# A recurrent attention and MLP kernel: unit 4's f, q and k turned by DMA transposes, and the first units in another order

## The chip, the cores and the metric

The kernel runs on one core of a Trainium2 chip. The metric is device microseconds of one execution; the time before is the median of seven runs.

## The reference

The input holds q, k, v and f_logit of shape (4, 8, 768, 48): 4 batches, 8 heads, 768 steps, 48 channels. An attention with a state that decays per channel is followed by a normalisation and a two-layer MLP with a residual.

```python
f = 1.0 / (1.0 + np.exp(-f_logit))
for t in range(S):
    state = f[:, :, t, :, None] * state + np.einsum('bhd,bhe->bhde', k[:, :, t], v[:, :, t])
    y[:, :, t] = np.einsum('bhd,bhde->bhe', q[:, :, t], state)
...
xn = (x - mu) / np.sqrt(var + 1e-06) * g_ln
ch = np.maximum(xn @ w_ch1, 0.0) @ w_ch2
return (x + ch)
```

Here x is y with the heads put side by side, (4, 768, 384); w_ch1 is 384 x 1536 and w_ch2 1536 x 384. The weights arrive as 64-bit floats and are turned into 32-bit floats on the chip; everything is computed in float32.

## The kernel before

**Units.** The 768 steps are cut into 12 units of 64 steps; a unit holds all 4 batches, so it has 256 rows for the MLP, and two batches fill the 128 partitions. The loop over units carries `state`. Within a unit the recurrence is written with cumulative products of the gates, made by two scans on VectorE (`after`, line 654, and `upto`, line 666, some 2.3 us each): the scaled k (`kh`, lines 673 and 708) and scaled q (`qh`, lines 673 and 716) give scores (line 751), these are masked (`sc`, line 755) and multiplied with v (line 777); the state of earlier units comes in through `carried` (line 737); `chunk` (line 807) and `state` (line 815) bring the state forward. `kt` (lines 767 and 769) is kh turned back for `chunk`.

**Two ways to get f, q and k with channels on the partitions.** A unit below `DIRECT` loads them as they lie and TensorE transposes them (`across`, line 646): 8 transposes of 128x128 each for f, k and q. A unit from `DIRECT` on takes another way. `split` (lines 424 to 436) lets ScalarE copy each half of the raw tile into two planes of 16-bit halves (line 432) and sends these to DRAM by a DMA on GpSimd's queue (line 436); `transfer` (lines 438 to 449) brings them back by a transposing DMA on SyncE's queue (line 448) into the tiles `turned` and, for k, into the raw tile of q. There is one `turned` for f and q, so the transfers of a unit have to follow each other's readers.

**The MLP.** `turn` (lines 834 to 844) transposes the normalised rows `xn` (line 830) into `xt`. Units 0 and 1 multiply plainly: six tokens of two column blocks of the first layer (`ph`, line 954, relu on ScalarE, line 956), and six tokens of four row blocks of the second (`po`, line 964). From unit 2 on the second layer uses a scheme with seven products (`pp`, line 983), with sums of h (lines 871 to 874) and mixed weights (`mix`, line 581); from unit 3 on the first layer uses a scheme with block products (`bw`, `bx`, `by`, `bz`, `bv`, line 892) and mixed weights (`mix_step`, line 607).

**The weights.** Each of the two matrices comes in 6 pieces of 768 KB. `fetch` issues a piece's DMA on SyncE's queue into one of two buffers (line 530); `read` lets ScalarE take it apart into `upper` and `units` (lines 542 and 543, 0.9 us each), each with two buffers; `write` puts it together on VectorE (lines 551, 554 and 556) and GpSimd (line 558). A piece is named by its first row or column: pieces 0 to 1280 of w1, pieces 0 to 10 of w2.

**What sets the order.** Every engine works through its own instructions in order, and their order is written out by hand in two strings. `START` covers units 0 to 2 and the attention up to unit 4, `UNIT` is repeated for each later unit. `run` (lines 1033 to 1061) goes through the tokens: `a2.q` is a stage of unit 2's attention, `m1` the next step of unit 1's MLP, `l3f` a load (four DMAs on SyncE's queue), `p5k0` a `split` of one half, `x5k` a `transfer`, `f`, `r` and `w` are fetch, read and write of the next weight piece, `d` is an idle matmul that only keeps TensorE busy (line 572), `T` and `t` one third of the mixing of w2 on GpSimd or VectorE, `U` and `u` a step of the mixing of w1, `s` the sums of h and `y` those of xt. A token puts its instructions at the end of the queues of all the engines that it uses, so where a token stands decides what waits behind what on each of them. PSUM gives the transposes and products four single banks in turn, so a product also waits until the reader of an earlier one is done. A DMA on SyncE's queue uses one of eight semaphores in turn and waits for the DMA that used it before.

Of the kernel before, what the change touches and what calls it, by code (L numbers as in the profile page):

```python
# [303 lines left out]


START = """
a0.gates l0k l0q f d a0.after l0x d r l0v d a0.upto
d f a0.kx l1f a0.k a0.kept l1k d a0.q f a0.carried a0.scores
a0.causal a0.values l1x l1q w r d a0.stats a0.kt f a1.gates w
d d a0.norm d a1.after l1v a0.chunk a0.turn f a0.state a1.upto m0  # L310
a1.kept r w a1.kx f a1.k m0 a1.q f r a1.kt r
w a1.carried a1.scores a1.causal d f l2k f l2v f w m0
a1.values r a1.stats l2f r a1.chunk w m0 a1.norm d l2x m0
a1.turn r m0 m1 r w w f w r m1 w
l2q m1 a1.state m1 a2.gates a2.after r m1 a2.kx f m0 m0
r w a2.k l3k w a2.upto a2.kept m1 a2.q m0 m0 m0
m0 a2.carried l3q a2.scores l3v l3f m1 l3x a2.causal U a2.values a2.stats
a2.norm m1 m1 m1 a3.gates m1 m1 a2.kt a2.turn a2.chunk a3.kx m2
m2 l4f a3.after a3.k m2 U a3.upto U T a2.state U a3.q
a3.kept m2 a3.carried a3.scores a3.kt l4v l4k a3.causal U a4.gates U U  # L320
U l4q T t U a3.values a3.chunk a4.after m2 l5f l5v U
a3.stats m2 a4.kx U a3.norm s2 m2 p5f0 a3.state l5k m2 a4.k
U m2 p5f1 m2 a4.kt u a3.turn l6f x5f p5k0 a4.upto a4.q
l4x p5k1 y3 l5q a5.gates m2 m2 l5x a4.kept m2
"""
UNIT = """
a{o}.after m{m} m{m} a{n}.carried a{n}.scores p{o}q0 m{m} a{n}.causal m{m} m{m} m{m} p{o}q1
# [8 lines left out]
def kernel(  # L336
# [19 lines left out]
    nc = tc.nc  # L356
    B, H, S, D = q.shape
    P = 128
    T = 64
# [12 lines left out]
    LEAST = 1e-12  # L372
    PLAIN = 2
    FIRST = 3
    DIRECT = 5
    PIECE = 768

    outer = ctx.enter_context(tc.tile_pool(name="outer", bufs=1))
# [28 lines left out]
    for name, fill in (("f", 40.0), ("q", 0.0), ("k", 0.0)):  # L407
        t = consts.tile([P, G, H, 64], FP32, name=f"{name}raw")
# [9 lines left out]
    halved = {}  # L418

    def raw_of(n, name):  # L420

        return wide_heads["k" if n >= DIRECT and name == "q" else name]

    def split(n, name, g):

        if n >= NU or n < DIRECT:
            return
        if (n, name) not in halved:
            halved[n, name] = drams.tile([P, 2, G, 64 * H], U16, tag=f"{name}halves",
                                         name=f"{name}halves{n}")  # L430
        planes = raws.tile([P, 2, 64 * H], U16, tag="planes", name=f"{name}planes{n}_{g}")
        nc.scalar.copy(  # L432
            out=planes,
            in_=raw_of(n, name)[:, g].rearrange("p h e -> p (h e)").bitcast(U16).rearrange(
                "p (c two) -> p two c", two=2))
        nc.gpsimd.dma_start(out=halved[n, name][:, :, g], in_=planes)  # L436

    def transfer(n, name):

        if n >= NU or n < DIRECT:  # L440
            return
# [188 lines left out]
    def attention(n):  # L630
# [7 lines left out]
        def new(name, shape, **kw):  # L638
            at[name] = work.tile(shape, FP32, tag=name, name=f"{name}{n}", **kw)
            return at[name]  # L640

        def across(src, g):

            pt = one_bank(f"tr{n}")
            for a in range(NP):
                nc.tensor.transpose(pt[:, a * P:(a + 1) * P],  # L646
                                    src[:, g, 2 * a:2 * a + 2].rearrange("p h e -> p (h e)"),
                                    ident)
            return pt.rearrange("p (s t) -> p s t", t=T)
# [20 lines left out]
        def times(dst, pts, by):  # L670
            for g, pt in enumerate(pts):
                segs = slice(g * HS, (g + 1) * HS)
                nc.vector.tensor_tensor(out=dst[:, segs], in0=pt, in1=by[:, segs, 1:E1],
                                        op=ALU.mult)

        def do_gates():
            new("after", [P, NS, E1])
            new("upto", [P, NS, E1])
            new("total", [P, NS], bufs=2)
            if n >= DIRECT:  # L680
                nc.scalar.activation(out=gv[:, :, 1:E1], in_=turned["f"], func=AF.Sigmoid)  # L681
# [17 lines left out]
        def do_k_across():  # L699
            if n < DIRECT:  # L700
                at["pk"] = [across(loaded[n, "k"], g) for g in range(G)]

        def do_k():
            kh = new("kh", [P, NS, T])
            if n < DIRECT:
                times(kh, at["pk"], at["after"])
# [326 lines left out]
    def run(plan):  # L1033
        for token in plan.split():
            kind, rest = token[0], token[1:]
            if kind == "a":
                n, stage = rest.split(".")
                if int(n) >= NU:
                    continue
                if "a" + n not in running:  # L1040
                    running["a" + n] = attention(int(n))
                running["a" + n].pop(stage)()
            elif kind == "m":
                if token not in running:
                    running[token] = mlp(int(rest))
                next(running[token])
            elif kind == "l":
                load(int(rest[:-1]), rest[-1])
            elif kind == "p":
                split(int(rest[:-2]), rest[-2], int(rest[-1]))  # L1050
            elif kind == "x":
                transfer(int(rest[:-1]), rest[-1])
            elif kind == "s":
                sums(int(rest))
            elif kind == "y":
                if FIRST <= int(rest) < NU:
                    sums_of_x(int(rest))
            else:
                {"r": read, "w": write, "f": fetch, "t": mix, "d": idle,
                 "T": lambda: mix(nc.gpsimd), "u": mix_step,  # L1060
                 "U": lambda: mix_step(nc.gpsimd)}[token]()
# [53 lines left out]
```

## Time and profile before

| what | value |
|---|---|
| median of 7 runs | 452.42 us |
| lowest and highest run | 448.65 and 453.76 us |
| the profiled execution | 451.44 us |
| span of its core | 449.7 us |
| around the span | 1.7 us |
| mean granted TensorE clock | 0.992 |
| chain of waits, by engine | PE 90%, DMA 3%, DVE 3% |
| HBM read and written | 30.67 and 15.73 MB |

PE is TensorE's matmuls, PEld its weight loads, DVE VectorE, ACT ScalarE, POOL GpSimd, SP SyncE. A line of a timeline has the start in us, the length in us, engine, source line, operation, output and input, their shapes, how many instructions are merged, and in brackets the idle time before them and what ended it. The chain of waits is followed back from the last instruction; its lines have the start, the length, and what the time went to.

### The profile page before, as it was taken

To read this page: it belongs to the slowest core of one execution; us is meant where nothing else is said; L and a number is where in the kernel's file an instruction comes from. 1 tells how busy PE (TensorE), PEld (TensorE's weight loads), DVE (VectorE), ACT (ScalarE), POOL (GpSimd) and SP (SyncE) were. 2 spreads that over 40 slices of the span, in tenths; PEclk is the share of its full clock that TensorE was granted. 3 is DMA by queue.
4 is the path that set the end of the run, shared out by engine and by line. 5 is a ranking of instruction groups with operands and counts; after the bars stand their busy time and mean duration, and the time that the engine had idled before them with its cause. 6 is when DMAs were issued, how large, how long until landed. Compare 5 with 4: busy or idle time off the path is not lost.

```text
span 449.7 us, 12979 instructions
## 1 busy us (share of the span) xinstructions
PE 432.4 (96%) x5487; PEld 401.8 (89%) x5487; DVE 330.0 (73%) x528; ACT 185.9 (41%) x333; POOL 126.8 (28%) x151
## 2 busy tenths in 40 slices
PE   5789999999999999999999999999999999999994
PEld 4568887667899999999999999999999999999994
DVE  6689878553678987888878878778778788565461
ACT  2266754003234445455454454464464451341320
POOL 2213543249715124124024024024024013011020
PEclk9899999999999999999999999999999999999998
DMA  8989997063645758777876767776778550000001
GB/s 136 196 186 249 244 210 137 20 128 62 121 79 127 182 123 195 153 159 180 148 167 168 152 147 184 159 158 167 160 132 203 118 118 19 21 1 18 20 10 34
DMA packets 173011, 58.36 MB, mean 130 GB/s; under 512 B 160784, under 2 KB 166416, under 8 KB 172944
## 3 DMA queue, kind: packets, MB, share of 16 engines
q1 hardware_dynamic: 167808, 46.03, 51.8%
q0 software_dynamic: 3360, 11.01, 6.8%
q8 instruction: 45, 0.74, 0.7%
q10 hardware_dynamic: 1776, 0.40, 0.5%
q14 instruction: 22, 0.18, 0.1%
HBM read 30.67 MB, written 15.73 MB: 103 GB/s over the span
## 4 chain that ended last, share of the span: by engine, by line
PE 90%; DMA 3%; DVE 3%; SPq 2%; issue 0%; ACT 0%
PE pp L983 30%; PE bx L892 12%; PE ph L954 9%; PE by L892 9%; PE po L964 7%; PE bz L892 4%; PE py L777 3%; PE py L737 3%; PE ps L751 2%; PE kp L767 2%; PE pn L807 2%; PE bv L892 2%; PE tr L646 2%; PE bw L892 2%; SPq L469 2%; PE xp L840 2%
## 5 line engine op out<-in xcount | busy, mean ns | idle before, releaser
L903 ACT ACTIVATE h<-h 128x512 f32<-128x512 f32 x45 | 28.3, 629 | 53.5 <-DVE h L900 47.4
L954 PE MATMUL ph<-xt,w 128*128 128x256 f32 x216 | 48.7, 380 | 0.8 <-ACT xt L842 0.8
L954 PEld LDWEIGHTS ph<-xt,w 128*128 128x128 f32 x216 | 40.4, 190 | 6.5 <-issue 1.0
L983 PE MATMUL pp<-mixed,h 128*128 128x192 f32 x240 | 42.4, 326 | 0.0
L983 PE MATMUL pp<-mixed,s 128*128 128x192 f32 x240 | 42.0, 326 | 0.0
L983 PE MATMUL pp<-w,h 128*128 128x192 f32 x240 | 40.7, 326 | 0.0
L983 PEld LDWEIGHTS pp<-mixed,h 128*128 128x128 f32 x240 | 39.5, 190 | 0.3 <-ACT xt L842 0.3
L983 PEld LDWEIGHTS pp<-mixed,s 128*128 128x128 f32 x240 | 39.1, 190 | 0.0
L983 PEld LDWEIGHTS pp<-w,h 128*128 128x128 f32 x240 | 38.8, 190 | 0.0
L436 POOL DMA_DIRECT2D qhalves<-qplanes x14 | 9.6, 683 | 97.8 <-ACT qplanes L432 97.8
L654 DVE TENSOR_TENSOR_SCAN after<-gates,ends 128x1040 f32<-128x1040 f32 (+1 forms) x13 | 28.7, 2211 | 6.3 <-ACT gates L686 3.4
L900 DVE TENSOR_TENSOR h<-h,bx 128x512 f32<-128x512 f32 x27 | 18.5, 687 | 18.8 <-PE bx L892 18.8
L964 PE MATMUL po<-w,h 128*128 128x384 f32 x96 | 32.0, 488 | 0.0
L666 DVE TENSOR_TENSOR_SCAN upto<-gates,starts 128x1040 f32<-128x1040 f32 (+1 forms) x13 | 30.1, 2314 | 0.4
L892 PE MATMUL bx<-y,v 128*128 128x128 f32 x216 | 29.4, 279 | 0.0
L900 DVE TENSOR_TENSOR h<-h,by 128x512 f32<-128x512 f32 x36 | 24.6, 683 | 6.3 <-PE by L892 5.0
L964 PEld LDWEIGHTS po<-w,h 128*128 128x128 f32 x96 | 17.8, 190 | 11.5
L892 PEld LDWEIGHTS bx<-y,v 128*128 128x128 f32 x216 | 26.2, 192 | 0.5
L681 ACT ACTIVATE gates<-turned 128x1024 f32<-128x1024 f32 x7 | 7.4, 1057 | 44.5 <-DMA turned<-fhalves 42.7
L842 ACT ACTIVATE xt<-xp,gain 128x128 f32<-128x128 f32 x72 | 19.9, 377 | 9.6 <-PE xp L840 9.6
L755 DVE TENSOR_TENSOR sc<-ps,causal 128x1024 f32<-128x1024 f32 x12 | 14.7, 1222 | 11.2 <-PE ps L751 11.2
L558 POOL TENSOR_TENSOR w<-w_0upper,w_0units 128x768 int32<-128x768 int32 x7 | 12.7, 1818 | 31.5 <-DVE w_0upper L556 26.3
(161 smaller groups left out, 960.2 us busy)
## 6 DMA issues: line engine op xcount, KB each, us to landing
w_0words<-in_moe_w_ch_dram SPq DMA_DIRECT2D x7, 768.0 KB, 5.5
kraw<-in_k_dram SPq DMA_DIRECT2D x48, 96.0 KB, 3.6
v<-in_v_dram SPq DMA_DIRECT2D x48, 96.0 KB, 3.0
fraw<-in_f_logit_dram SPq DMA_DIRECT2D x46, 96.0 KB, 3.5
fhalves<-fplanes POOLq DMA_DIRECT2D x14, 256.0 KB, 3.0
khalves<-kplanes POOLq DMA_DIRECT2D x14, 256.0 KB, 2.9
qhalves<-qplanes POOLq DMA_DIRECT2D x14, 256.0 KB, 3.1
kraw<-in_q_dram SPq DMA_DIRECT2D x28, 96.0 KB, 3.2
```

The lines of the kernel that those rows point to most:

```text
L654: nc.vector.tensor_tensor_scan(out=at["after"].rearrange(flat)[:, c0:c1][:, ::-1], data0=gt[:, c0 + 1:c1 + 1][:, ::-1], data1=ends.rearran ...
L666: nc.vector.tensor_tensor_scan(out=at["upto"].rearrange(flat)[:, c0:c1], data0=gt[:, c0:c1], data1=starts.rearrange(flat)[:, c0:c1], initi ...
L737: nc.tensor.matmul(py[half(b), r, e * D:(e + 1) * D], lhsT=qh[head_rows(r), 2 * e + b], rhs=kept[head_rows(r), b, e], start=e == 0, stop=F ...
L755: nc.vector.tensor_tensor(out=new("sc", [P, 2, GA, T]).rearrange("s r e t -> s (r e) t"), in0=at["ps"].rearrange("s r e t -> s (r e) t"), ...
L777: nc.tensor.matmul(py[half(b), r, e * D:(e + 1) * D], lhsT=sc[rows, r, e], rhs=vx[rows, g, a] if r else vt[rows, g, 2 * a], start=n == 0 a ...
L842: nc.scalar.mul(out=xt[:, m, g * P:(g + 1) * P], in_=pt[:, m], mul=gain[:, m:m + 1])
L892: nc.tensor.matmul(banks[bank][:, i], lhsT=right[:, i * P:(i + 1) * P], rhs=left, start=new and i == 0, stop=True, skip_group_check=True)
L900: nc.vector.tensor_tensor(out=out[to], in0=out[to], in1=bank, op=op)
L903: nc.scalar.activation(out=out[to], in_=out[to] if bank is None else bank, func=AF.Relu)
L954: nc.tensor.matmul(ph[:, j], lhsT=w1[:, m, (i + j) * P:(i + j + 1) * P], rhs=xt[:, m], start=m == 0, stop=m == KD - 1)
L964: nc.tensor.matmul(po, lhsT=h[:, i, g * P:(g + 1) * P], rhs=w2[:, i], start=i == 0, stop=i == KF - 1)
L983: nc.tensor.matmul(pp, lhsT=a[:, i], rhs=b[:, i], start=i == 0, stop=i == KH - 1)
```

## The change

Three edits. `DIRECT` is 4 instead of 5: unit 4 is the first whose f, q and k are split and turned by transfers. The DMA that sends the halves to DRAM is issued on ScalarE's queue for that unit; for later units it stays on GpSimd's. And `START` is written anew: it has the splits and transfers of unit 4 (`p4f0` to `p4q1`, `x4f`, `x4k`, `x4q`), no `a4.kx`, 8 idle matmuls instead of 11, `T` three times where it was `T` twice and `t` once, and the other tokens in another order. `UNIT` is the same.

```diff
 START = """
-a0.gates l0k l0q f d a0.after l0x d r l0v d a0.upto
-d f a0.kx l1f a0.k a0.kept l1k d a0.q f a0.carried a0.scores
-a0.causal a0.values l1x l1q w r d a0.stats a0.kt f a1.gates w
-d d a0.norm d a1.after l1v a0.chunk a0.turn f a0.state a1.upto m0
-a1.kept r w a1.kx f a1.k m0 a1.q f r a1.kt r
-w a1.carried a1.scores a1.causal d f l2k f l2v f w m0
-a1.values r a1.stats l2f r a1.chunk w m0 a1.norm d l2x m0
-a1.turn r m0 m1 r w w f w r m1 w
-l2q m1 a1.state m1 a2.gates a2.after r m1 a2.kx f m0 m0
...
-m2 l4f a3.after a3.k m2 U a3.upto U T a2.state U a3.q
-a3.kept m2 a3.carried a3.scores a3.kt l4v l4k a3.causal U a4.gates U U
-U l4q T t U a3.values a3.chunk a4.after m2 l5f l5v U
-a3.stats m2 a4.kx U a3.norm s2 m2 p5f0 a3.state l5k m2 a4.k
-U m2 p5f1 m2 a4.kt u a3.turn l6f x5f p5k0 a4.upto a4.q
-l4x p5k1 y3 l5q a5.gates m2 m2 l5x a4.kept m2
+a0.gates l0k a0.kx l0q d d f a0.after a0.upto l0v l0x r
+f a0.k d d l1f a0.q a0.kept a0.carried d a0.scores a0.causal l1k
+w d a0.values r a0.stats d f l1x a0.kt f l1q a0.norm
+f l1v w a1.gates a1.after a0.chunk a0.turn a0.state f a1.upto r m0
+r a1.kept r a1.kx m0 w a1.k a1.q a1.kt w a1.carried a1.scores
+a1.causal f l2k f m0 w a1.values a1.stats r l2v d f
+l2f w a1.norm m0 m0 f r w f a1.chunk a1.turn m0
+a1.state r r m1 r w f w m1 m1 m1 a2.gates
+w a2.after m0 r l2x w a2.kx r m0 a2.k m1 w
...
+m2 a3.upto m1 p4f1 m1 l4k p4k0 x4f T T U p4k1
+a3.q l4q a2.state T m1 U m2 a3.kept l4v U a3.carried a3.scores
+U U p4q0 a3.kt a4.gates l5f m2 x4k a3.causal a3.chunk U a3.values
+p4q1 a4.after a3.stats l5k l5v m2 U x4q m2 a3.norm s2 a3.turn
+p5f0 m2 U a4.upto m2 p5f1 m2 a3.state a4.k p5k0 a4.q m2
+x5f U a4.kt p5k1 l4x u y3 l5q m2 l5x a4.kept a5.gates
+m2 m2 l6f
 """
...
-    DIRECT = 5
+    DIRECT = 4
...
-        nc.gpsimd.dma_start(out=halved[n, name][:, :, g], in_=planes)
+        (nc.scalar if n == DIRECT else nc.gpsimd).dma_start(out=halved[n, name][:, :, g], in_=planes)
```

More of the change, by code (lines that the diff above doesn't have):

```diff
@@ L306 @@
 START = """
-a0.gates l0k l0q f d a0.after l0x d r l0v d a0.upto
-d f a0.kx l1f a0.k a0.kept l1k d a0.q f a0.carried a0.scores
-a0.causal a0.values l1x l1q w r d a0.stats a0.kt f a1.gates w
-d d a0.norm d a1.after l1v a0.chunk a0.turn f a0.state a1.upto m0
-a1.kept r w a1.kx f a1.k m0 a1.q f r a1.kt r
-w a1.carried a1.scores a1.causal d f l2k f l2v f w m0
-a1.values r a1.stats l2f r a1.chunk w m0 a1.norm d l2x m0
-a1.turn r m0 m1 r w w f w r m1 w
-l2q m1 a1.state m1 a2.gates a2.after r m1 a2.kx f m0 m0
-r w a2.k l3k w a2.upto a2.kept m1 a2.q m0 m0 m0
-m0 a2.carried l3q a2.scores l3v l3f m1 l3x a2.causal U a2.values a2.stats
-a2.norm m1 m1 m1 a3.gates m1 m1 a2.kt a2.turn a2.chunk a3.kx m2
-m2 l4f a3.after a3.k m2 U a3.upto U T a2.state U a3.q
-a3.kept m2 a3.carried a3.scores a3.kt l4v l4k a3.causal U a4.gates U U
-U l4q T t U a3.values a3.chunk a4.after m2 l5f l5v U
-a3.stats m2 a4.kx U a3.norm s2 m2 p5f0 a3.state l5k m2 a4.k
-U m2 p5f1 m2 a4.kt u a3.turn l6f x5f p5k0 a4.upto a4.q
-l4x p5k1 y3 l5q a5.gates m2 m2 l5x a4.kept m2
+a0.gates l0k a0.kx l0q d d f a0.after a0.upto l0v l0x r
[7 more added lines that the diff above has]
+w a2.after m0 r l2x w a2.kx r m0 a2.k m1 w
+a2.upto l3k m1 l2q l3f U l3x a2.q m0 a2.kept m0 m0
+l3q a2.carried a2.scores m0 m1 a2.causal a2.values U a2.stats m1 l3v a3.gates
+a2.kt a2.norm l4f m1 a3.after a2.turn p4f0 a2.chunk a3.kx m2 a3.k U
+m2 a3.upto m1 p4f1 m1 l4k p4k0 x4f T T U p4k1
[5 more added lines that the diff above has]
+m2 m2 l6f
 """
```

## The prediction

> **What bounds the kernel now.** I read the engine shares first, then stretches of 10 us, then the chain of waits, then single engines' timelines.
>
> ```profile
> span 449.7 us, 12979 instructions
> PE 432.4 (96%) x5487; PEld 401.8 (89%) x5487; DVE 330.0 (73%) x528; ACT 185.9 (41%) x333; POOL 126.8 (28%) x151
> ```
>
> TensorE is busy for 432.4 of 449.7 us. The stretches (columns: length, then busy us of PE, PEld, DVE, ACT, POOL, then granted clock, DMA share, GB/s) show where the other 17.3 us lie:
>
> ```profile
> 10.00:20.00 10.00, 7.30 (x151) 6.09 (x150) 8.05 (x14) 2.54 (x4) 1.30 (x1) 0.94 0.88 216
> 20.00:30.00 10.00, 7.48 (x96) 5.49 (x95) 7.39 (x10) 5.58 (x13) 3.35 (x4) 0.89 0.98 192
> 30.00:40.00 10.00, 9.52 (x175) 8.43 (x173) 9.69 (x16) 5.98 (x9) 1.84 (x1) 1.00 0.98 232
> 40.00:50.00 10.00, 10.00 (x173) 8.71 (x165) 9.22 (x14) 7.01 (x10) 6.32 (x5) 1.00 0.65 204
> 50.00:60.00 10.00, 10.00 (x51) 8.84 (x50) 7.01 (x9) 6.44 (x13) 4.32 (x3) 1.00 1.08 260
> 60.00:70.00 10.00, 10.00 (x55) 8.63 (x54) 8.03 (x7) 5.75 (x9) 3.64 (x2) 1.00 1.10 197
> ```
>
> With 5.0 us of idle time in the first 10, 10.7 us are lost before 40 us (and 22 passes of idle matmuls, 0.48 us each in the median, fill part of the rest) and 6.7 after 400. Between, TensorE never waits: there only removed TensorE work, or a new wait, moves the end. Before 40 us the chain shows what the first products wait for:
>
> ```profile
> 15.62 6.93 DMA w_256words<-in_moe_w_ch_dram
> ...
> 25.64 2.28 DVE xn L830 x2
> 27.91 2.24 DVE after L654
> ...
> 30.68 2.33 DVE upto L666
> ```
>
> VectorE works in order: xn of unit 0 stands behind the writing of weight piece 256 and so behind that piece's DMA, though its own input was ready (variance on POOL) at 22.1 us.
>
> I sum at three marks of before: M1, the first product with unit 1's xt (51.65 us); M2, the end of the third token of po (80.15); M3, unit 3's first block product (151.15). After M3 the orders are the same and TensorE is full, so what is won by M3 is won in the end.
>
> **Part 1, to M1: xn of unit 0 ahead of the second piece.** xn takes 2.36 us above, beside a POOL write; a later one takes 0.86 with POOL still. It now fits into VectorE's idle 2.47 us (21.0 to 23.49), ending at 23.0. Then ScalarE sets the pace: units of piece 256 end at 24.27, kt at 25.2, the two gates at 26.2, six xt copies 1.66: the first ph starts at about 27.7 instead of 29.35. On VectorE, after starts at 26.2 (was 27.83), upto ends 31.25, kept 32.1, piece 512 is written by 34.1, kh by 35.3 (was 37.1). Reading piece 512 now stands ahead of the first relu on ScalarE, so it is read at its landing (29.0, issue 23.93 and 5.1) and not at 32.71; piece 1024 is requested at some 31.4 instead of 34.5.
> Then the DMA decides. Piece 1280 landed at 43.6 (issue 38.07, landing 5.5). The same bytes precede it in both orders, and DMA was at 0.98 until 40, so I leave it at 43.6: read (0.9 to the first half), written on VectorE (2.1), xn (2.36, beside POOL again) put xn of unit 1 at 49.0. TensorE comes there at 48.4: ph at 27.7, 31.2, 38.2, 42.3 and 44.9, carried at 36.8, pn to 48.4. So M1 falls at 49.4: **2.25 us won**; 0 if piece 1280 lands 2.25 us later.
>
> **Part 2, M1 to M2: reads ahead of relus.** On ScalarE the reads of w2's pieces 4 and 6 now stand before the relus of unit 1's products 2 to 4. The second half of the f transposes of unit 2 needs the bank of product 2, so it waits for piece 6 of w2. Before, that read began at 61.12, waiting for its DMA:
>
> ```profile
> 61.12 0.93 ACT L542 ACTIVATE w_0upper<-w_0words 128x768 f32<-128x768 f32 x1 [1.88 <-DMA w_0words<-in_moe_w_ch_dram]
> 61.95 0.91 ACT L543 ACTIVATE w_0units<-w_0words 128x768 int32<-128x768 uint32 x1
> 62.75 1.06 ACT L956 ACTIVATE h<-ph 128x512 f32<-128x512 f32 x2
> ```
>
> The relu was over 2.25 us after the landing, and TensorE needed it at 65.0: 1.7 us of cover. Now TensorE comes at 62.75, and f of unit 2 is requested ahead of the piece. From 43.6 on, 4.32 MB are ahead of its landing (four pieces of 0.786, three inputs of 0.393). At 260 GB/s (the stretch 50 to 60, which has this mix) it lands at 60.2; at 197 (60 to 70) at 65.5. I take 250: 60.9, a wait of 0.4. Then q of unit 2 is requested behind k of unit 3, and that behind unit 2's k transposes and the last weight piece: landing about 75.0 against 74.6, another 0.4. M2: **1.45 us won** (78.7).
>
> **Part 3, M2 to M3: unit 4 by transfers.** Removed: 24 transposes, three groups of 8, each 0.87 us from start to start (133.92 to 134.80): 2.6 us off a full TensorE. Added: six ScalarE copies (1.0 each) and six DMA issues on ScalarE (two took 1.42 at the start, 0.71 each), 10.3 us on an engine busy 2.7 to 4.9 of each 10 us between 100 and 150; by my order kt of unit 3 is still copied 1.7 us before pn needs it. If that cover went, pn would wait one for one. Three transfers on SP issue in 2.0 to 2.9 us and land in 4.4 to 5.4 (7.0 at most): by my order f lands 4 us before its sigmoid, k 9 and q 4 before use, with loads in front of them counted. One mix goes from VectorE (2.0) to POOL (4.0): from 16.4 us after M2 POOL has 7 steps of 1.3 and 12 of 1.0, so it ends at 37.5, and the first product that needs them starts 56 after M2. Loads, sigmoids and multiplies keep their lengths (kh 1.27 for two halves, 1.21 whole).
> But a new wait comes. upto of unit 4 moves ahead of kh on VectorE, and the transposes of kh stand after the fourth pp:
>
> ```profile
> 134.75 0.96 DVE L871 TENSOR_TENSOR s<-h 128x768 f32<-128x768 f32 x1 [0.16 <-ACT h L956]
> ...
> 138.77 0.94 DVE L815 TENSOR_TENSOR state<-kept,pn 128x768 f32<-128x768 f32 x1
> 139.63 0.34 DVE L991 TENSOR_TENSOR p1x<-p1x,pp 128x192 f32<-128x192 f32 x1
> 139.90 1.27 DVE L673 TENSOR_TENSOR kh<-tr,after 128x512 f32<-128x512 f32 x2
> ```
>
> From the end of unit 2's last ph: sums from 0.83 to 4.85, upto 2.73 (160.66 to 163.39), two adds 0.54, state 0.87, kh 1.2: 10.2. TensorE has xp 0.7 and four pp 7.8 and stands at 8.5. It waits 1.7 us. Net of part 3: **0.9 won**, 2.6 without that wait.
>
> **The three idle matmuls less, and k ahead of others.** The granted clock fell to 0.50 from 19 to 22 us, after gaps; kp took 1.91 us there and 1.04 warm. With three idles less between f of unit 1 and pn, TensorE is busy about 3.1 of the 4.3 us before the first ph. If that ph ran slower by 1.91 to 1.04 it would cost 2.2 us, of which 0.6 are covered by xn of unit 1; at 1.00 nothing. I take nothing, since the clock recovered by itself after 22 us.
> [...]
>
> **Sum.** 1.45 + 0.9 = 2.4 us: 449.0 in the profiled execution's terms (451.44). That one lies 1 us below the median of the seven runs, 452.42; the forecast for a median is **450.0**. A measurement can tell about 0.5% (2.3 us) from no change.
>
> **Rivals.**
> 1. *The waits do not come* (w2 lands at 60, kh is ready by 8.5 us): for, the 260 GB/s stretch; against, VectorE's order, which is fixed. 2.25 + 2.6 = 4.9 won: 447.6.
> 2. *Only the transposes pay*: the first ph runs cold or piece 1280 is 1.5 us late, so 0 to 0.5 is left at M2; with 0.9 that is 451.3. For: clock 0.50; against: clock 1.00 from 25 us.
> 3. *Slower: TensorE waits for piece 6 of w2 through the relus.* At 197 GB/s it lands at 65.5, the wait is 5.0 and the late last piece delays q by 0.6: 2.25 - 5.6 + 0.9 = -2.4, so 454.9. It decides below some 215 GB/s (landing after 63.7). For: 192 and 197 in two stretches full of inputs; against: those carried more small inputs.
> 4. *ScalarE's queue holds the transfers*: if q's transfer is over 4 us late, VectorE stops at qh with the adds behind it; each us costs one. It ends on rival 3's side. That the change does not do what it says is out: in the built order unit 4 has no transposes of f, k and q.
>
> **Chances.** Forecast 0.40, rival 1 0.15, rival 2 0.25, rival 3 0.16, rival 4 0.04. Most of the forecast's case, and rival 1, lie beyond 0.5%: faster 0.48; same 0.32 (rival 2 and the forecast's shallow side); slower 0.20. The range runs from rival 1, less 0.9 for the spread of the runs, to rival 3: 446.7 to 454.9.
>
> **What would show it.** First ph near 27.7; M1 near 49.4; f transposes of unit 2 split by a wait of under 1 us; no unit 4 transposes of f, k and q; a wait of about 1.7 us ahead of kp of unit 4, put down to kh; M3 near 148.8 and 33.2 us per unit as before. I am wrong if TensorE waits over 2 us for a relu near 63 us, if a transfer is what VectorE waits for near 140, or if the stretch 20 to 35 shows a clock below 0.89.

## The result and the profile after

The changed kernel takes 454.05 us in the median of 25 runs against 451.27 us of 62 runs of the kernel before: a ratio of 1.0063, interval 1.0048 to 1.0078. A second measurement gave 453.94 against 452.14 us, 1.0034 (1.0002 to 1.0065). The two medians differ by 0.6% and 0.4%, and both intervals lie above 1: it is slightly slower, where 450.0 and faster had been forecast. Each ratio and its interval compare the two sets of runs and can differ a little from the quotient of the two medians. The profiled execution has a span of 451.9 us (449.7 before). First the page of the changed kernel, then its stretches with the columns of the prediction:

```profile
span 451.9 us, 12930 instructions
PE 432.0 (96%) x5457; PEld 400.1 (89%) x5457; DVE 334.4 (74%) x522; ACT 191.8 (42%) x338; POOL 131.8 (29%) x155
```

```profile
20.00:30.00 10.00, 8.84 (x107) 7.17 (x100) 7.79 (x11) 7.69 (x17) 4.98 (x4) 0.75 1.23 249
...
140.00:150.00 10.00, 6.99 (x37) 6.72 (x36) 9.93 (x14) 3.16 (x4) 5.08 (x7) 0.83 0.46 120
```

TensorE has fewer matmuls and is busy as long as before (432.0, 432.4). The stretch from 140 us shows why: TensorE idles for 3.0 us and has a granted clock of 0.83 of full speed, while VectorE is busy for 9.93 of 10. The marks divide the difference:

| distance, us | before | changed |
|---|---|---|
| start to M1 | 51.65 | 51.77 |
| M1 to M3 | 99.50 | 101.37 |
| M3 to the end | 298.55 | 298.76 |

M1 is the first product behind the transposes of unit 1's xn; the instruction there is unit 0's last first-layer product, so it is a mark and not a reader of xt. Nothing is won up to M1 (2.25 was forecast), and 1.87 us are lost from M1 to M3, where about 0.1 was to be won (0.9 less the two waits of 0.4).

**Up to M1.** The early xn came as forecast: 0.87 us instead of 2.36, and the scan `after` started at 26.32 (26.2 forecast). Right behind it the gain was lost. VectorE, then GpSimd in this profile:

```profile
26.32 2.32 DVE L655 TENSOR_TENSOR_SCAN after<-gates,ends 128x1040 f32<-128x1040 f32 x1
28.67 1.62 DVE L664 TENSOR_SCALAR total<-after 128x16 f32<-128x16 f32 x1
```

```profile
26.55 3.70 POOL L559 TENSOR_TENSOR w<-w_256upper,w_256units 128x768 int32<-128x768 int32 x1 [3.10 <-DVE w_256upper L557]
```

The addition takes 1.8 us elsewhere. It started during the scan, which ends at 28.64, and ended 1.6 us after that, at 30.25; `total`, 0.17 us in the kernel before, ended at 30.29. So the addition seems to wait for the scan, and `total` for the addition.

Which instruction pays differs from profile to profile. In five of the eleven profiles with the new early order (runs 7 and 13 left out) it is `total`, with 1.60 to 1.62 us. In the other six the scan itself takes 2.98 to 3.73 us. There, by my estimate, `after` starts behind the addition: in the first profile the addition starts 1.11 us behind the start of VectorE's last step for piece 256 (25.44 to 26.55), and elsewhere it takes 1.82 us. In the second profile of the changed kernel that step starts at 24.78, so the addition would run from 25.89 to 27.71:

```profile
26.66 3.23 DVE L655 TENSOR_TENSOR_SCAN after<-gates,ends 128x1040 f32<-128x1040 f32 x1 [0.92 <-ACT gates L687]
29.93 0.18 DVE L664 TENSOR_SCALAR total<-after 128x16 f32<-128x16 f32 x1
```

From the start of `after` to the start of `upto` it is 2.85 us in the kernel before and 3.5 to 4.3 in these eleven profiles.

**M1 to M2.** ScalarE's read of piece 6 of w2, and TensorE's f transposes of unit 2 that were to wait for the relu behind it:

```profile
62.34 0.91 ACT L543 ACTIVATE w_0upper<-w_0words 128x768 f32<-128x768 f32 x1 [2.66 <-DMA w_0words<-in_moe_w_ch_dram]
```

```profile
64.72 1.04 PE L647 MATMUL tr<-ident,fraw 128*128 128x128 f32 x8
```

All eight transposes run together, with no idle time ahead of them. From M1 to the xn transposes of unit 2 it is 49.31 to 49.33 us in the eleven profiles that have the new order up to there (not run 4, whose order is the old one by then, nor run 13 with 49.42), with M1 between 50.35 and 54.47, so nothing waits there.

**M2 to M3.** VectorE, GpSimd and TensorE of the changed kernel around the kp of unit 4, the TensorE transposes that turn its kh back:

```profile
137.69 1.90 DVE L664 TENSOR_SCALAR total<-after 128x16 f32<-128x16 f32 x1
...
139.91 2.33 DVE L667 TENSOR_TENSOR_SCAN upto<-gates,starts 128x1040 f32<-128x1040 f32 x1
...
142.66 0.95 DVE L816 TENSOR_TENSOR state<-kept,pn 128x768 f32<-128x768 f32 x1
143.52 1.22 DVE L709 TENSOR_TENSOR kh<-qraw,after 128x1024 f32<-128x1024 f32 x1
```

```profile
138.19 1.35 POOL L608 TENSOR_TENSOR v<-v,w 128x512 f32<-128x512 f32 x1
```

```profile
144.89 1.94 PE L768 MATMUL kp<-ident,kh 128*128 128x128 f32 x8 [3.01 <-DVE kh L709]
146.62 2.78 PE L984 MATMUL pp<-mixed,h 128*128 128x192 f32 x12
```

This is the wait that the prediction named, with 3.0 us instead of 1.7: `total` ends when GpSimd's step on v does, 1.7 us late. Behind the wait TensorE is cold, that is, it runs at a lower granted clock (0.83 from 140 to 150 us, 1.00 in the kernel before): kp takes 1.94 us (1.04 before), the next product 2.78 (2.11), together another 1.57.

### The profile page after: what moved, and what is told of

It reads as the page before. It is cut to its first block, busy times and chain, and to the rows that moved or that the text cites. A ratio compares the mean times of both kernels' runs of the same rounds, so it can differ in the third digit from the quotient of the medians.

```text
span 451.9 us, 12930 instructions
## 1 busy us (share of the span) xinstructions
PE 432.0 (96%) x5457; PEld 400.1 (89%) x5457; DVE 334.4 (74%) x522; ACT 191.8 (42%) x338; POOL 131.8 (29%) x155
## 4 chain that ended last, share of the span: by engine, by line
PE 87%; SPq 4%; DVE 4%; DMA 2%; issue 1%; ACT 0%; POOL 0%; DVEq 0%
PE pp L984 29%; PE bx L893 12%; PE by L893 9%; PE ph L955 8%; PE po L965 7%; PE bz L893 4%; SPq L470 3%; PE py L778 3%; PE py L738 3%; PE kp L768 2%; PE ps L752 2%; PE pn L808 2%; PE bv L893 2%; PE bw L893 2%; PE xp L841 1%; DMA turned<-qhalves 1%
## 5 line engine op out<-in xcount | busy, mean ns | idle before, releaser
L655 DVE TENSOR_TENSOR_SCAN after<-gates,ends 128x1040 f32<-128x1040 f32 (+1 forms) x13 | 30.2, 2322 | 7.4 <-ACT gates L682 4.1
L901 DVE TENSOR_TENSOR h<-h,bx 128x512 f32<-128x512 f32 x27 | 18.5, 687 | 18.6 <-PE bx L893 18.6
L682 ACT ACTIVATE gates<-turned 128x1024 f32<-128x1024 f32 x8 | 8.5, 1059 | 43.1 <-DMA turned<-fhalves 43.1
L433 ACT COPY fplanes<-fraw 128x1024 uint16<-128x1024 uint16 x16 | 16.8, 1051 | 12.4 <-issue 12.4
```

What stands on the lines that cost most here:

```text
L433: nc.scalar.copy(out=planes, in_=raw_of(n, name)[:, g].rearrange("p h e -> p (h e)").bitcast(U16).rearrange("p (c two) -> p two c", two=2))
L655: nc.vector.tensor_tensor_scan(out=at["after"].rearrange(flat)[:, c0:c1][:, ::-1], data0=gt[:, c0 + 1:c1 + 1][:, ::-1], data1=ends.rearran ...
L901: nc.vector.tensor_tensor(out=out[to], in0=out[to], in1=bank, op=op)
```

## The experiments

The theory to test (A): the early gain is eaten by VectorE's own order, and the loss is made at the kp of unit 4 by `upto` ahead of kh, with GpSimd's steps lengthening VectorE. The rivals: B, the transfers and ScalarE's queue cost the time; C, the new early order does.

| kernel | median / before on the same chip | ratio (interval) | M1 | M1 to M3 | M3 to end |
|---|---|---|---|---|---|
| 1 kh first | 452.75 / 451.22 | 1.0029 (1.0004 to 1.0055) | 50.83 | 98.28 | 300.59 |
| 2 one step later | 451.15 / 451.22 | 1.001 (0.9979 to 1.0041) | 50.35 | 98.67 | 298.58 |
| 3 old start | 461.3 / 451.22 | 1.022 (1.0166 to 1.0273) | 53.00 | 105.58 | 298.52 |
| 4 new start alone | 452.31 / 451.22 | 1.0011 (0.9984 to 1.0037) | 52.05 | 99.60 | 298.55 |
| 5 upto last | 451.58 / 451.37 | 1.0001 (0.9974 to 1.0028) | 52.24 | 96.69 | 301.47 |
| 6 GpSimd's queue | 458.98 / 451.37 | 1.0157 (1.0117 to 1.0198) | 52.44 | 106.20 | 299.06 |
| 7 one addition less | 452.41, one run | | 50.60 | 101.22 | 298.78 |
| before, again | 452.14, one run | | 52.58 | 99.51 | 298.21 |
| 8 steps early | 452.0 / 452.14 | 1.001 (0.9983 to 1.0038) | 51.56 | 98.68 | 298.86 |
| 9 steps early, upto last | 454.81 / 452.14 | 1.0018 (0.9981 to 1.0054) | 54.47 | 96.68 | 303.35 |
| 10 before, steps early | 452.09 / 452.14 | 1.0002 (0.9975 to 1.0029) | 49.87 | 100.77 | 298.36 |
| changed, again | 453.94 / 452.14 | 1.0034 (1.0002 to 1.0065) | 52.98 | 101.57 | 299.45 |
| 11 = 9, load early | 450.27 / 451.83 | 0.997 (0.9947 to 0.9994) | 51.71 | 96.69 | 298.70 |
| 12 = 11, last step late | 450.42 / 451.83 | 0.997 (0.9949 to 0.9992) | 51.35 | 96.69 | 301.16 |
| 13 = 12, norm first | 451.43 / 451.83 | 0.9985 (0.9966 to 1.0003) | 52.97 | 96.78 | 298.35 |

M1 moves by up to 4 us from profile to profile of one order, so the two other distances tell more than a span. The times of 9 lie far apart, from 449.8 to 456.8 us; its profiled execution took 456.3.

**1. kh ahead of upto.**

```diff
-p5f0 m2 U a4.upto m2 p5f1 m2 a3.state a4.k p5k0 a4.q m2
+p5f0 m2 U a4.k a4.upto m2 p5f1 m2 a3.state p5k0 a4.q m2
```

> The changed kernel with one move: kh of unit 4 on VectorE ahead of total, reciprocal and upto of unit 4 (in the changed kernel it stands behind them). Theory A (the loss is made by this order: TensorE stands 3.0 us before the kp of unit 4 for kh, and then runs kp in 1.94 us instead of 1.04 and the next product in 2.78 instead of 2.11): the wait goes, kp takes about 1.04, M3 (153.14 in the changed kernel) comes 3.0 + 0.9 + 0.7 = 4.5 us earlier, at 148.6, and the time falls from 454.05 to about 449.5; anything up to 451 still speaks for it, if part of the wait turns up at qh. Theory B (the load of the ten added transfers on the DMA engines and on ScalarE's queue is what makes kh late): kh cannot run earlier, the wait stays at 2 us or more and the time at 453 to 455. Theory C (the new order of the first units is the loss): no change, 454.

M1 to M3 fell by 3.1 us, not 4.5, and 1.8 came back behind M3. TensorE's waits in this run (total, times, longest):

```profile
PE kp L768 <- DVE p1x L992: 1.4, 1, 1.4
PE bz L893 <- ACT h L898: 1.0, 1, 1.0
...
PE bx L893 <- DVE u4y L992: 0.6, 1, 0.6
```

Theory A was right about the cause of the wait and too simple about its cure: what stands behind `upto` is late whatever it is. kp now waits for a bank that the p1x sum reads. And kh itself, now beside GpSimd's step on v, took 2.98 us instead of 1.22.

**2. GpSimd's step on v later.**

```diff
-p5f0 m2 U a4.upto m2 p5f1 m2 a3.state a4.k p5k0 a4.q m2 x5f U a4.kt
+p5f0 m2 a4.upto m2 p5f1 m2 a3.state a4.k p5k0 a4.q m2 x5f U a4.kt U
```

> The changed kernel with one move: the GpSimd step that writes a v block (1.35 us, started at 138.19) is taken from ahead of upto of unit 4 to behind the kp of unit 4. Nothing on VectorE is reordered. [...] Theory B (transfers): total shrinks but the wait before kp stays near 3.0, 454. [...]

`total` took 0.69 us (1.90 in the changed kernel), and the wait shrank by 1.2 us, where theory B had it stay near 3.0:

```profile
PE kp L768 <- DVE kh L709: 1.8, 1, 1.8
```

kp ran warm (1.06 us; clock 1.00 from 140 to 150 us). GpSimd's step is the reason for the long `total`.

**3 and 4. The two halves of the change apart.** Up to `a2.norm` one kernel's order, from there the other's; 4 has `DIRECT = 5`.

> The first units in the order of the kernel before, up to xn of unit 2 (its three more idle matmuls too), then the order of the changed kernel, with unit 4 by transfers. Theory A: the first product with unit 1's xt comes at 51.7 in both orders, so nothing changes: 453.5 to 454.6, with the wait of about 3 us before the kp of unit 4 still there. Theory C (the new order of the first units costs, for instance by the colder clock of 0.75 from 20 to 30 us): the time falls below 452.

> The first units in the order of the changed kernel up to xn of unit 2, then the order of the kernel before, with unit 4 transposed on TensorE. Theory A: the new order of the first units is worth nothing by itself: 451.3 within 0.8, with no wait before the kp of unit 4. Theory C: 453.5 or more. The forecast's own parts 1 and 2 would give 451.3 - 3.7 = 447.6.

Run 3 does not answer: f of unit 3 now landed late (TensorE waited 2.88 and 0.61 us for it near 102 us). Its wait before kp was 3.03 us again. Run 4 does: the new early order alone is worth nothing that can be measured (the 3.7 us of the forecast's first two parts, a ratio of 0.992, lie outside its interval), and M1 to M3 is that of the kernel before.

**5. upto behind kh and the sums,** as in the kernel before.

```diff
-p5f0 m2 U a4.upto m2 p5f1 m2 a3.state a4.k p5k0 a4.q m2
+p5f0 m2 U m2 a3.state a4.k p5f1 m2 p5k0 a4.upto a4.q m2
```

> The changed kernel with VectorE's order around unit 4 put back as in the kernel before: state of unit 3, kh of unit 4, one partial sum, and only then total, reciprocal and upto. Theory A: moving kh alone ahead of upto only moved the wait on (kp waited 1.4 us for the p1x sum, later products 1.0 and 0.6); with the sums ahead of upto too, no wait is left, M1 to M3 falls from 101.4 us to 99.5 - 2.6 = 96.9 (24 transposes less than before), and M3 to the end stays at 298.6. That is 4.3 less than the changed kernel, about 449.8, a ratio of 0.996 to 0.998 to the kernel before. Theory B (the transfers themselves cost): M1 to M3 stays above 98.5 and the ratio at 1.0 or more.

M1 to M3 is 96.69 as forecast: the transposes pay there, 2.81 us. But 2.9 us more than in the kernel before passed behind M3, and the time is that of the kernel before, not the 449.8 expected:

```profile
PE bx L893 <- DVE u4y L992: 1.4, 1, 1.4
...
PE bz L893 <- ACT h L898: 0.8, 1, 0.8
```

The prediction's rule that what is won by M3 is won in the end does not hold.

**6. The halves on GpSimd's queue.**

```diff
-        (nc.scalar if n == DIRECT else nc.gpsimd).dma_start(out=halved[n, name][:, :, g], in_=planes)
+        nc.gpsimd.dma_start(out=halved[n, name][:, :, g], in_=planes)
```

> The changed kernel with the halves of unit 4 sent on GpSimd's queue, as those of all later units are, instead of ScalarE's. Theory A: the queue plays no part; the wait before the kp of unit 4 stays at about 3.0 us and the time within 0.3% of the changed kernel's 454. Theory B (ScalarE's queue holds the transfers or ScalarE's copies up): the wait falls below 1.5 and the time below 452.

Both theories were wrong: it is 5 us slower than the changed kernel. GpSimd's and VectorE's timelines:

```profile
136.71 0.79 POOL L437 DMA_DIRECT2D qhalves<-qplanes  x1
137.58 0.22 POOL L796 TENSOR_SCALAR rstd<-mv 128x2 f32<-128x2 f32 x1
```

```profile
138.64 1.81 DVE L831 TENSOR_SCALAR xn<-x,mv,rstd 128x384 f32<-128x384 f32 x2 [7.88 <-POOL rstd L797]
```

The variance was ready at 130.75, but on GpSimd rstd stood behind the mixing and the issues, and some of these had waited for ScalarE's copies (7.35 us at 105 us). TensorE waited 6.1 us for that xn and was cold behind it (six transposes 1.51 us instead of 0.82, the clock at 7 tenths from 137.3 to 148.8 us on the page). ScalarE's queue is the part of the change that works.

**7. One addition less on GpSimd, and the kernel before again.** In 7 VectorE's last step for piece 256 writes `to` instead of `upper`, and GpSimd's addition is left out.

> The changed kernel, in which GpSimd's addition of the low words is left out for the second piece of the first weight (columns 256 to 511 lose their last bits; VectorE writes them straight to the weight tile). Theory A for the early part (what the earlier xn won on VectorE is lost two instructions later, where the 16-column total waits for GpSimd's addition to end, 1.62 us instead of 0.17, the addition itself having waited for the scan): total takes 0.2, and from the first statistics of unit 0 to the kh of unit 1 VectorE takes 13.4 us instead of 14.86. The first product behind the transposes of unit 1's xn comes 29.6 to 30.4 us after those statistics instead of 30.9. Rival (a weight piece or x decides there): the distance to that product stays at 30.9 although total is short.

> The kernel before, unchanged, for a second profile. The first statistics of unit 0 stood at 19.58 us before, and at 20.90, 19.43, 19.48 and 20.20 in four profiles of the new order of the first units, following the issue of the last input of unit 0 on SyncE's queue, which took 5.30, 3.59, 3.83 and 4.89 us there and 4.31 before. If that is jitter of the start and not the order, this profile shows an issue of 3.5 to 5.5 us and the statistics moved by as much; from the statistics to the product behind unit 1's transposes it should be 32.1 us again, against 30.9 to 31.9 in the new order.

VectorE of 7, whose line numbers are up to four further:

```profile
28.21 0.18 DVE L668 TENSOR_SCALAR total<-after 128x16 f32<-128x16 f32 x1
```

From the first statistics to kh it is 13.42 us (14.86 in the changed kernel), and 30.16 to M1 (30.87), both as forecast. So the addition costs 1.4 us up to kh, and 0.7 of it is left at M1, in one profile each. The second profile of before shows the jitter: SyncE's last issue of unit 0 took 3.52 us, the statistics came at 18.37, and yet M1 at 52.58. Its distance from the statistics, 34.2 us, was not the 32.1 expected: VectorE stood 2.25 us ahead of kh there for ScalarE's reading of piece 512, which the old order puts behind the first relu. So the statistics alone do not set M1. Over all profiles of each order (four of the old one with 3 and 10, eleven of the new one without 7 and 13), in means:

| stretch | old order | new order |
|---|---|---|
| to the first statistics of unit 0 | 19.15 | 19.80 |
| to kh of unit 1 | 16.80 | 15.34 |
| to the first statistics of unit 1 | 9.17 | 9.86 |
| to M1 | 6.65 | 6.97 |
| M1 (lowest and highest) | 51.8 (49.9 to 53.0) | 52.0 (50.4 to 54.5) |

In these means 1.46 us are won up to kh and 1.66 lost, 0.65 ahead of the statistics and 1.0 behind kh. The split is rough, since the second row alone runs from 14.92 to 18.39 in the four profiles of the old order; that M1 comes no earlier is plain, and run 4 agrees. In the old order the third row is 9.17 in every profile; in the new one it is 9.05 to 12.20. The 12.20 is run 9, where the first product of unit 0's MLP ran cold (the clock at 5 tenths from 22.7 to 34.1 us on the page):

```profile
29.75 5.07 PE L955 MATMUL ph<-xt,w 128*128 128x256 f32 x12 [0.69 <-ACT xt L843]
```

In all other profiles that product took 2.83 us. Why the rest (9.05 to 10.42, and the later statistics), the runs don't settle.

**8, 9 and 10. GpSimd's last three steps on v where GpSimd is idle,** ahead of the values of unit 3 (the lines that lose the steps are left out here); in 9 with the move of 5, in 10 in the kernel before. Theory A2, which A becomes here: from the sums of unit 2 to the scores of unit 4 VectorE is the bound (busy without a gap for 22.3 us in run 1), and it takes longer beside GpSimd's steps (`total` 1.90 us, 0.69 in run 2).

```diff
-U U p4q0 a3.kt a4.gates l5f m2 x4k a3.causal a3.chunk U a3.values
+U U p4q0 a3.kt a4.gates l5f m2 x4k a3.causal a3.chunk U U U U a3.values
```

> The changed kernel, VectorE's order untouched, with the last three GpSimd steps on v (1.3 us each; they started at 131.2, 138.2 and 148.0) moved to where GpSimd is idle, ahead of the values of unit 3 (some 123 to 128 us). [...] Theory B (the transfers on their own cost time): the ratio stays at 1.005.

> Both moves together: the three GpSimd steps early, and upto of unit 4 behind kh and the sums. Theory A2: no wait before the kp of unit 4, and the wait of 1.4 us behind M3 for the u4y sum, which the second move alone had left, goes as well, since VectorE's stretch from the sums of unit 2 to the scores of unit 4 falls from 21.4 to about 19 us and is shorter than TensorE's. M1 to M3 96.8, M3 to the end 298.6: 4.6 less than the changed kernel, 449.0 within 0.7, a ratio of 0.993 to 0.997: the 24 transposes then pay in full, 2.6 us. Theory B: 451 or more.

> The kernel before with its last three GpSimd steps on v moved to the same place, no transfers for unit 4. Theory A2: in the kernel before TensorE is the bound in this stretch (VectorE has idle gaps of 1.44 and 0.79 us there), so a shorter VectorE wins nothing: M1 to M3 99.5, ratio 0.998 to 1.002. If instead the ratio falls to 0.996 or less, the steps pay by themselves, and what the combination wins is not owed to the transfers.

> The changed kernel, unchanged, on the same chip as these three. Ratio to the kernel before 1.004 to 1.008 by the earlier measurement. What is asked of its second profile: whether the kp of unit 4 behind its 3.0 us wait runs cold again (1.94 us and 2.78 for the next product in the first profile; 1.06 in the profile of the old start, with the same wait). Cold: M1 to M3 101.4. Not cold: about 99.9.

In 8 `total` took 0.69 us, the five y sums 2.37 (3.31 in the changed kernel), the wait was 1.8, M1 to M3 98.68, and the ratio 1.001, where theory B had 1.005. 10 won nothing, as forecast in its ratio; its profile had a wait of 0.9 us for a weight piece. 9 missed: the wait for u4y fell from 1.4 to 0.4, and another one came. ScalarE and TensorE in 9:

```profile
167.89 1.04 ACT L433 COPY fplanes<-fraw 128x1024 uint16<-128x1024 uint16 x1 [3.48 <-DMA fraw<-in_f_logit_dram]
```

```profile
169.48 1.16 PE L893 MATMUL bz<-y,w 128*128 128x128 f32 x8 [2.13 <-ACT h L898]
170.47 1.58 PE L893 MATMUL bx<-y,v 128*128 128x128 f32 x8
171.85 1.91 PE L893 MATMUL by<-y,v 128*128 128x128 f32 x8
```

ScalarE's copy of f of unit 6 waits for its load, the emptying of a bank stands behind it, TensorE waits for the bank and is cold afterwards (clock 0.83 from 170 to 180 us). In the kernel before that load was issued at 141.25 us, in the changed one at 160.89: the new order puts `l6f` last. The changed kernel does not show it, because its TensorE comes late enough (copy at 165.62, no wait). The changed kernel again: the 3.02 us wait is cold a second time.

```profile
146.12 1.36 PE L768 MATMUL kp<-ident,kh 128*128 128x128 f32 x8 [3.02 <-DVE kh L709]
147.27 3.55 PE L984 MATMUL pp<-mixed,h 128*128 128x192 f32 x12
```

**11. The load of f of unit 6 early; 12. VectorE's own step on v late; 13. xn of unit 1 ahead of the sixth piece.**

```diff
-p5k0 a4.upto a4.q m2 x5f a4.kt p5k1 l4x u y3 l5q m2 l5x a4.kept a5.gates m2 m2 l6f
+p5k0 a4.upto a4.q m2 l6f x5f a4.kt p5k1 l4x u y3 l5q m2 l5x a4.kept a5.gates m2 m2
```

In 12 `u` goes from ahead of `y3` to the end; in 13, besides, `w a1.norm` becomes `a1.norm w`.

> The combination of the two earlier moves (GpSimd steps early; upto of unit 4 behind kh and the sums), and in addition the loading of f of unit 6 is issued ahead of the transfer of f of unit 5, as in the kernel before, instead of at the end of the list. In the combination ScalarE's copy of f of unit 6 waited 3.5 us for that load (167.9 us), a product's eviction stood behind it on ScalarE, and TensorE waited 2.1 us for its bank and ran at a clock of 0.83 in the next 10 us. Theory A3 (once TensorE runs early, the load that the new order puts last is the next bound): that wait and the cold stretch go, M1 to M3 stays at 96.7 and M3 to the end falls from 303.4 to 298.6 to 299.0: together 395.3 to 395.7 against 398.05 of the kernel before, 2.4 us won, ratio 0.993 to 0.997. Rival (VectorE is the bound behind M3 anyway): M3 to the end stays above 300.5, ratio 0.999 or more.

> The same, and VectorE's own last step on v (0.68 us) goes behind the sums and y sums of unit 3 instead of ahead of them. Theory A3: the wait of 0.4 us for the u4y sum behind M3 goes too, the y sums end 0.7 us earlier; 0.4 us less than the run before it, ratio 0.992 to 0.996. If VectorE's order no longer matters there: the same as that run within 0.2.

> The same as the run before it, and in the first units xn of unit 1 stands ahead of the writing of the sixth weight piece on VectorE, instead of behind it, where it took 2.36 us beside GpSimd's addition (0.87 alone). [...] Rival (TensorE's own work or a landing decides there): no change within 0.2.

11 is faster than the kernel before by 0.3%, the upper end of the interval just below 1 (0.9994), and its median lies some 3.7 us below those of the changed kernel, which were measured apart from it. M1 to M3 and M3 to the end sum to 395.4 us (398.05 before, 400.1 changed), as forecast. TensorE at the kp of unit 4, no longer with idle time ahead, and the one wait left behind it:

```profile
141.67 1.04 PE L768 MATMUL kp<-ident,kh 128*128 128x128 f32 x8
142.54 2.12 PE L984 MATMUL pp<-mixed,h 128*128 128x192 f32 x12
```

```profile
PE bx L893 <- DVE u4y L992: 0.4, 1, 0.4
```

12 is no faster than 11, as the rival had it. Its wait for u4y is gone, and in its profile a copy of q waited for a load in the same way:

```profile
154.68 1.04 ACT L433 COPY qplanes<-kraw 128x1024 uint16<-128x1024 uint16 x1 [3.08 <-DMA kraw<-in_q_dram]
```

In 13 xn of unit 1 takes 0.87 instead of 2.36, and yet M1 is no earlier (33.3 us behind the first statistics), and unit 0's last product waits 0.4 us for the sixth piece there. So xn alone does not set M1. No run has the early load without the other two moves of 11, so it is not shown whether all three are needed.

## Why the prediction was wrong

- **Part 1, 2.25 us won up to M1: wrong, 0 measured.** The step that failed is the chain from "after starts at 26.2" to "upto ends 31.25" and kh at 35.3: both instructions were taken at their lengths of before. GpSimd's addition of piece 256, which xn no longer met, now met `total` or `after` and cost 0.7 to 1.45 us in every profile of the new order; without it kh came 1.4 us earlier (run 7). The prediction moved an instruction out of a collision and did not ask what would stand in it next. What takes the rest stays open. It also read the bound from one profile; M1 moves by 4 us, and "then the DMA decides" was no more than one of several chains.
- **The three idle matmuls less, taken at nothing: right in the changed kernel.** The first product took 2.83 us there, as before. The sign set for the opposite, a clock below 0.89 from 20 to 35 us, came all the same (0.83), but the low clock was over before that product (0.50 from 20 to 25 us, 0.99 from 25 to 30; the product starts at 28.18). In run 9 alone the product was cold, 2.24 us longer, close to the 2.2 that the prediction had priced; whether the three idle matmuls would have prevented that is not shown.
- **Part 2, two waits of 0.4 us: did not come.** Rival 3 (piece 6 of w2 through the relus) did not either.
- **Part 3, 24 transposes, 2.6 us: right.** 2.81 in runs 5, 9 and 11.
- **Part 3, the new wait of 1.7 us: right mechanism, mis-sized.** It is 3.0, since `total`, reciprocal and `upto` took 4.55 us and not 2.73 (the last sum ahead of them took 0.4 less than in the kernel before). And 1.6 to 1.8 of cold TensorE follow in the two profiles of the changed kernel, a term that the sum did not have: the clock was asked about only for the idle matmuls of the start. Of GpSimd's steps the prediction asked only when they end, not what they hold up on VectorE. 2.8 - 3.0 - 1.6 accounts for 1.8 of the 1.87 lost.
- **"Transfers land early": right for unit 4, but not the whole of it.** No transfer of unit 4 held anything. What was missed is the load of f of unit 6 behind all of it, and VectorE: from the sums of unit 2 on it is busy without a gap for 18.6 us in the changed kernel, and for 22.3, to the scores of unit 4, in run 1. With TensorE's work shortened by 2.8 us VectorE, and then ScalarE's copies, are the bound. That is where the 2.8 us went in runs 5 and 9, and what was regained up to M3 in run 1; run 11 has both out of the way and got 2.7 us in its profile and 1.6 in the median.
- **Rivals 1 and 2.** Rival 1 assumed no waits and fell with the kp. Rival 2, that only the transposes pay, is right that nothing is left of the early part, but in the changed kernel neither of its reasons came: the first product was not cold, and the reading of piece 1280 waited for no transfer. Run 5 shows that taking the wait before kp away was not enough for the transposes to pay; run 11 comes nearest to this rival.
- **Rival 3's 454.9 is close to the 454.05 measured by chance:** its wait at 63 us did not come.
- **Rival 4** had the place right (ScalarE's queue), but not the case: it is the copies' wait for loads that holds the emptying of banks, and only in kernels with an earlier TensorE.
- **The sum.** Forecast 2.4 won; measured in the profiles 2.2 lost: 0.1 to M1, 1.9 to M3, 0.2 behind.

## What to carry to other kernels

When a full engine is relieved, ask at once who is next: count the busy time of the other engines in that same stretch, and look at every load that the new order issues later. Ask also what will stand where a moved instruction stood: here xn, moved away from GpSimd's addition (0.87 us instead of 2.36), left it to a tiny instruction (`total`, 1.62 instead of 0.17) or to the scan. A wait of 3 us on TensorE cost half as much again through the clock in three of four profiles here (1.4 to 1.8 us); a forecast should carry such a term.

## What was not expected of the hardware

- A 16-column operation on VectorE took 1.62 and 1.90 us beside GpSimd (0.17 alone), a GpSimd addition 3.70 beside a scan (1.8 alone), and a scan up to 3.73 (2.32 alone) where, by the estimate above, that addition had started first. So of the addition and what VectorE ran beside it the second to start was the longer one. The `total` of 1.90 us does not show this: it started at 137.69, ahead of the step on v (138.19, 1.35 us).
- Waits of 3.0 us left TensorE cold in three profiles of four with such a wait (the changed kernel twice and run 7: clock 0.83, 0.84 and 0.83 from 140 to 150 us; not in run 3, clock 1.00 from 150 to 160), one of 2.1 us did too (run 9, clock 0.83 from 170 to 180), and so did the 6.1 us of run 6; waits of 1.4 and 1.8 us in runs 1, 2 and 8 did not (the product behind kp took 2.12 us in each).
- The same four loads of unit 0 kept SyncE's queue for 3.59 to 5.42 us in profiles of the same order, and M1 followed only in part.
